# One attention-and-routing kernel: score groups moved together, mask diagonals split, routing moved, a float32 gather for two rows, dummy matmuls

## The chip, the cores and the metric

The kernel runs on one core of a Trainium2 chip. The metric is the device time of one execution in microseconds; before and after are compared by medians of several runs. All times in the rows below come from one profiled execution of the kernel before.

## The reference, cut to what matters

Three layers follow one another. Linear attention with decay, 2 batches, 8 heads, 768 tokens, 48 channels; a routed layer with 8 experts; a gated layer.

```python
# attention, per token t
cur = einsum('bhd,bhe->bhde', u * k_t, v_t);  y_t = einsum('bhd,bhde->bhe', r_t, state + cur)
state = w * state + einsum('bhd,bhe->bhde', k_t, v_t)
# experts: x = y as 1536 x 384
e = argmax(x @ w_gate);  gate_w = softmax(x @ w_gate)[e]
disp[e, position of the token among those of e] = x
out = gate_w * (relu(disp @ w1[e]) @ w2[e])
# gated layer
(sigmoid(out @ w_gate2) * (out @ w_val)) @ w_out
```

## The kernel before, in words

**Attention** works in eight steps `s`, one for each batch and pair of heads (s = 0 to 3 are batch zero, 4 to 7 batch one), over 768 tokens in six chunks of 128. The schedule is written out by hand: every engine runs its own instructions in the order of the program, and the loop `for s in range(8)` interleaves the work of several steps. In the turn `s` of the loop stand

- `a_mm(s+1, C0)` and `a_mm(s+1, C1)`: the scores of chunks 0 to 3 and 4 to 5 on PE, into two PSUM buffers (`ap`);
- `u_pe(s+1)`: products of decayed keys (`kkd`, made on POOL by `kk_part`) with values, on PE; `u_scan(s+1)`: the scan over chunks on DVE, which gives the states `ts`;
- `a_cp(s+1, ...)`: a predicated copy on DVE of the scores above the diagonal into the matrix `at`;
- `sums(s+2)`: the diagonal's values `dl` on DVE, from products that POOL makes (`pr_part`); `diag(s+2, js)`: for each of twelve 128x128 blocks an ACT instruction that writes identity times `dl` into `at`;
- `rp(s+2)` and `kb(s+2)`: the scaling of queries and keys (`dm`) on DVE, which the scores of the next turn need;
- `y_part(s, 2)`, `y_part(s+1, 0)`, `y_part(s+1, 1)`: outputs of two chunks each on PE, from the states and from `at`; `out_evac`: their copy from PSUM to `yt` on ACT;
- `out_tr(s)`: transposition and gate logits on PE (six float32 matmuls of 136 columns, which the trace shows as twelve instructions); `out_x(s)`: copy of the transposed rows to `xs` on ACT; `out_l()`: addition of the logits to `lg` on DVE.

PSUM tiles named `big` rotate through three buffers: each turn takes four, `T1[s]`, `Y0[s+1]` and two `XP[s]`.

**Expert weights** are split into a high and a low part beside the attention: `bg(n)` takes n tiles `raw`, ACT makes `rh`, DVE makes `rl`. `BG` says how many in which turn. The rest follows in the expert stage.

**Routing.** `r1(b)` finds the expert of each token (maxima, differences, one-hot `oh` on DVE, an exponential `ex` on ACT, whose sum DVE takes), `cnt` counts, `r2(b)` ranks by small matmuls on PE, `r3(b)` makes positions and gates on DVE, `r4(b, c, eng)` scales 128 rows on DVE or ACT and scatters them from POOL's queue into the buffer `xs_d` in DRAM, by expert. Batch zero is routed in the turns 4 to 6 (`RS` says which rows are sent when). After the loop, `pre()` loads the rows of expert 0 that came from batch zero, behind all six scatters of batch zero, on SP's queue; batch one is routed, and `first()` gathers expert 0's rows of batch one straight from SBUF: `xr` is transposed by PE into `xk`, and then each of six row blocks, scaled and split into a high and a low float32r part (`hi` on ACT, `lo` on DVE), is multiplied by a selection matrix `pick` and added into `xk`. `xk` is split into `xeh` and `xel`, and the expert stage begins with `s1` (`ph`).

`warm_up(n)` issues n matmuls of zeros, 512 columns each.

**Behind it** the expert stage (`s1`, `s2`) and the gated layer (`mf`, `mo`) follow; the decoding of the gated layer's weights (`wa`) runs beside them.

Of the kernel before, what the change touches and what calls it, by code (L numbers as in the profile page):

```python
# [27 lines left out]
R4E = "vsvsvs"  # L28
W0 = 3
WD = 15  # L30
ZI = (0, 0, 2, 2, 2, 2, 0, 0)
NKR = 3
NV = 4
ND = 5
WARM = 22
BG = (0, 0, 1, 1, 1, 0, 2, 3)
DP = 2
NB = 224
NP = NB // 2
OB = 6  # L40
# [6 lines left out]
OVP = 60  # L47
NT = 2
TAILF = 2
R4A = [3, 5]  # L50
R4S = [3]
EB0 = (5, 6)
EB = (4, 6)
DMAX = (122880.0 - 2.0 ** -7) * 2.0 ** 16
# [54 lines left out]
def body(tc, A, out):  # L109
    nc = tc.nc  # L110
    E = mybir.EngineType
    with ExitStack() as top, tc.manual_schedule():
# [129 lines left out]
        with ExitStack() as ctx:  # L242
# [116 lines left out]
            def diag(s, js):  # L359
                at_tile(s)  # L360
                for j in js:
                    nc.scalar.mul(AT[s][:, j, :], ident, DL[s][:, j:j + 1])  # L362

            def u_pe(s):
                for c in range(5):
                    for h in range(2):
                        nc.tensor.matmul(ups[64 * h:64 * h + 64, s % 2, :, c], kkd[s % 2][:, c, h, :],
                                         V[s][:, (2 * c + h) * 48:(2 * c + h) * 48 + 48], start=True, stop=True)
# [6 lines left out]
            def a_mm(s, cs):  # L375
                ap = ps.tile([128, 2, 512], F32, tag="a", name="ap")[:, :, 0:128 * len(cs)]
                for i, c in enumerate(cs):
                    t = slice(c * 128, c * 128 + 128)
                    for h in range(2):
                        q = slice(64 * h, 64 * h + 48)  # L380
                        nc.tensor.matmul(ap[:, h, i * 128:i * 128 + 128], D[s][q, 1, t], D[s][q, 0, t], start=True, stop=True,
                                         skip_group_check=True)
                return ap
# [34 lines left out]
            def out_evac(s, g):  # L418
                if g == 0:
                    yts[s] = wp.tile([128, 768], F32, tag="yt", name="yt")  # L420
                if s == 7:
                    a, b, src = ((0, 256, y7.get(0)), (256, 512, y7.get(1)), (512, 768, T1.get(7)))[g]
                else:
                    a, b, src = ((0, 512, Y0[s]), (512, 768, T1.get(s)))[g]
                nc.scalar.copy(out=yts[s][:, a:b], in_=src[:, 0:b - a])
# [89 lines left out]
            def first():  # L515
                x, m2, oh, rank, pi, gk = R[1]
                xk = [pb.tile([128, 512], F32, tag="big", name="xk")[:, 0:NB] for _ in range(3)]
                for b in range(2):
                    for kt in range(3):
                        nc.tensor.matmul(xk[kt][:, b * NP:b * NP + NP], xr0[0][0:NP, b, kt * 128:kt * 128 + 128],  # L520
                                         ident[0:NP, 0:NP], start=(b == 0), stop=False, skip_group_check=True)
                pick = wp.tile([128, 12, 128], F32R, tag="at", name="pick", bufs=3).rearrange("p a b -> p (a b)")
                his = wp.tile([128, 12, 128], F32R, tag="at", name="his", bufs=3).rearrange("p a b -> p (a b)")
                los = wp.tile([128, 12, 128], F32R, tag="at", name="los", bufs=3).rearrange("p a b -> p (a b)")
                for c in range(6):
                    (nc.gpsimd if c > DP else nc.vector).tensor_scalar(
                        out=pick[:, c * NB:c * NB + NB], in0=cat[:, 512:512 + NB], scalar1=pfs[1][:, c:c + 1],
                        scalar2=None, op0=ALU.is_equal)
                hl = []
                for c in range(6):  # L530
                    if c < 4:
                        hi, lo = his[:, c * 384:c * 384 + 384], los[:, c * 384:c * 384 + 384]
                    else:
                        hi = xp_.tile([128, 384], F32R, tag="hi", name="hi", bufs=2)
                        lo = xp_.tile([128, 384], F32R, tag="lo", name="lo", bufs=2)
                    hl.append((hi, lo))
                    nc.scalar.mul(hi, x[:, c, :], gk[:, c:c + 1])
                    if c in R4A:
                        r4(1, R4A.index(c), "s")
                    nc.vector.scalar_tensor_tensor(out=lo, in0=x[:, c, :], scalar=gk[:, c:c + 1], in1=hi.bitcast(F32),  # L540
                                                   op0=ALU.mult, op1=ALU.subtract)
                order = [(c, kt, p) for b in (0, 2) for p in range(2) for c in (b, b + 1) for kt in range(3)]
                order += [(c, kt, p) for kt in range(3) for c in (4, 5) for p in range(2)]
                for c, kt, p in order:
                    nc.tensor.matmul(xk[kt], hl[c][p][:, kt * 128:(kt + 1) * 128], pick[:, c * NB:c * NB + NB],
                                     start=False, stop=(c == 5 and p == 1), skip_group_check=True)
                for c in range(len(R4A), 6):
                    r4(1, c, "s" if c in R4S else "v")
                for kt in range(3):
                    nc.scalar.copy(out=xeh[:, kt, :], in_=xk[kt])  # L550
                    nc.vector.tensor_sub(xel[:, kt, :], xk[kt], xeh[:, kt, :].bitcast(F32))

            def r4(b, c, eng):
                x, m2, oh, rank, pi, gk = R[b]
                if eng == "v":
                    nc.vector.tensor_scalar_mul(x[:, c, :], x[:, c, :], gk[:, c:c + 1])
                else:
                    nc.scalar.mul(x[:, c, :], x[:, c, :], gk[:, c:c + 1])
                scatter(scx, "scx", xs_d, pi[:, c:c + 1], x[:, c, :], 8 * 1536)

            def cnt(b):
                with nc.allow_low_precision("counts of at most six are exact"):
                    nc.vector.reduce_sum(out=cnts[:, b, :], in_=R[b][2].rearrange("p c e -> p e c"), axis=AX.X)
# [4 lines left out]
            def consts():  # L568
                nc.gpsimd.tensor_copy(out=tri, in_=cat[:, 0:128])
                nc.gpsimd.memset(ones, 1.0)  # L570
                nc.gpsimd.iota(tid, pattern=[[128, 12]], base=0, channel_multiplier=1)
                nc.gpsimd.tensor_copy(out=capf, in_=capi)
# [66 lines left out]
            y_part(0, 0)  # L639
            y_part(0, 1)  # L640
            out_evac(0, 0)

            for s in range(8):
                nx, fu = s < 7, s < 6
                fetch(sum(BG[:s + 2]))
                if s < 5:
                    load(s + 3, "k")
                    load(s + 3, "v")
                if s < 4:
                    load(s + 4, "d")  # L650
                for _ in range(ZI[s]):
                    zinit()
                if s == 4:
                    consts()
                if nx:
                    ap0 = a_mm(s + 1, C0)
                    u_pe(s + 1)
                if s == 5:
                    r2(0)
                y_part(s, 2)  # L660
                out_evac(s, 1 if nx else 2)
                subs = []
                bg(BG[s], False, 0, subs)
                if nx:
                    a_cp(s + 1, C0, ap0)
                    u_scan(s + 1)
                    ap1 = a_mm(s + 1, C1)
                    a_cp(s + 1, C1, ap1)
                for c in RS.get((s, 0), ()):
                    r4(0, c, R4E[c])  # L670
                if fu:
                    sums(s + 2)
                    diag(s + 2, range(12))
                for f in subs:
                    f()
                if fu:
                    rp(s + 2)
                    behind(kk_part(s + 2), kb(s + 2))
                    if s < 5:
                        pr_part(s + 3, P_)  # L680
                if s == 4:
                    r1(0)
                    cnt(0)
                if s == 5:
                    r3(0)
                if nx:
                    y_part(s + 1, 0)
                    if s == 6:
                        out_evac(7, 0)
                    y_part(s + 1, 1)  # L690
                    out_evac(s + 1, 1 if s == 6 else 0)
                    out_tr(s)
                    out_x(s)
                    out_l()
                    for c in RS.get((s, 1), ()):
                        r4(0, c, R4E[c])
            out_tr(7)
            out_x(7, True)
            pre()
            r1(1)  # L700
# [314 lines left out]
```

## Time and profile before

| | us |
|---|---|
| runs shown: median, lowest, highest | 473.31, 471.04, 473.49 |
| the profiled execution: its time, its span | 473.62, 471.9 |
| first score matmul of turn 0 (`a_mm(1)`) | 19.52 |
| the same in turns 1, 2, 3, 4, 5, 6 | 31.76, 39.59, 47.96, 55.91, 63.94, 77.51 |
| `xr` there, first matmul on it | 94.86 |
| first matmul of the expert stage | 103.07 |

How to read the rows: a row of the timeline has start and length in us, the engine, the line, the operation, what it writes and reads, the shape, how many instructions are merged, and in brackets how long the engine had been idle before it and who released it. Engines' instructions are pipelined, so a row's length is a little more than the distance to the next row. A row of stages has its bounds, its length, then the busy time and the count of PE, PE's weight loads, DVE, ACT and POOL, then the clock that was granted to PE as a share of 2.4 GHz (0.50 is 1.2 GHz), the busy share of the DMA engines, and GB/s. SPq is SP's DMA queue, with the moment of issue.

### The profile page before, as it was taken

The page shows a single profiled execution, that of the slowest core. Times are in us where ns is not written, and L with a number is a line of the kernel's source. Part 1 is how long each engine was busy: PE and PEld are TensorE (multiplying, and loading weights), DVE is VectorE, ACT ScalarE, POOL GpSimd, SP SyncE. Part 2 cuts the span into 40 slices and gives each one's busy share as a digit, 9 for nine tenths or more (in the row PEclk, how much of TensorE's full clock was granted, in tenths as well). Part 3 has the DMA queues.
Part 4 walks back from the last instruction along what each step waited for, and adds up shares of the span by engine and source line. Part 5 has one row for each costly group of instructions (what it writes and reads, how often), then busy time and mean ns, then how long its engine had stood idle before and what let it go on. Part 6 is the DMA issues. An engine that isn't in the chain of part 4 may idle for free.

```text
span 471.9 us, 8275 instructions
## 1 busy us (share of the span) xinstructions
PE 447.4 (95%) x3210; PEld 420.0 (89%) x3211; DVE 279.7 (59%) x504; ACT 218.0 (46%) x468; POOL 108.3 (23%) x103
## 2 busy tenths in 40 slices
PE   8899979499999999999999999999999999999994
PEld 4577857499999999999988999999899999999993
DVE  6747697748998999877277767675451212121211
ACT  3346756736776767775254443434243222222222
POOL 2533543570011101200023635313104000000013
PEclk9969997879999999999999999999999999999998
DMA  7999940468798788685023533522002000000002
GB/s 242 339 293 314 312 145 19 139 241 265 216 305 241 239 266 250 162 252 192 1 68 73 129 73 129 122 79 68 1 0 102 0 2 0 1 0 1 0 4 97
DMA packets 23194, 63.53 MB, mean 135 GB/s; under 512 B 4592, under 2 KB 8304, under 8 KB 23152
## 3 DMA queue, kind: packets, MB, share of 16 engines
q1 hardware_dynamic: 21088, 58.24, 40.9%
q0 software_dynamic: 1920, 4.73, 2.7%
q8 instruction: 26, 0.43, 0.4%
q14 instruction: 16, 0.13, 0.1%
q10 hardware_dynamic: 144, 0.00, 0.0%
HBM read 55.48 MB, written 7.48 MB: 133 GB/s over the span
## 4 chain that ended last, share of the span: by engine, by line
PE 29%; DVE 12%; ACT 7%; issue 4%; POOL 1%; POOLq 0%; ACTq 0%; DVEq 0%
PE pg L940 9%; PE po L963 9%; PE pv L940 9%; DVE sg L948 2%; DVE wa L175 2%; ACT wa L165 2%; DVE wa L168 2%; DVE wa L179 2%; ACT gh L949 1%; DVE wa L171 1%; DVE gl L950 1%; ACT rh L185 1%; PE ph L840 1%; ACT sg L946 1%; PE py L859 1%
## 5 line engine op out<-in xcount | busy, mean ns | idle before, releaser
L948 DVE TENSOR_TENSOR sg<-sg,pv 128x384 f32<-128x384 f32 (+2 forms) x49 | 26.7, 544 | 91.9 <-PE pv L940 78.7
L145 DVE TENSOR_TENSOR rl<-raw,rh 128x768 fp32r<-128x768 f32 x56 | 57.1, 1020 | 11.4 <-ACT rh L143 11.4
L859 PE MATMUL py<-hh,rh 128*128 128x448 f32 x192 | 63.5, 374 | 0.0
L949 ACT CAST gh<-sg 128x384 fp32r<-128x384 f32 (+2 forms) x49 | 24.8, 507 | 80.6 <-DVE sg L948 79.1
L143 ACT CAST rh<-raw 128x768 fp32r<-128x768 f32 x64 | 53.2, 836 | 16.0 <-PE py L859 12.0
L858 PE MATMUL py<-hh,rl 128*128 128x224 f32 x192 | 52.4, 273 | 0.0
L189 POOL TENSOR_TENSOR wy<-wa,wy 128x768 fp32r<-128x768 f32 x10 | 18.8, 1878 | 143.6 <-ACT wy L185 143.6
L946 ACT ACTIVATE sg<-pg 128x384 f32<-128x384 f32 x48 | 23.4, 488 | 50.6 <-PE pg L940 50.6
L950 DVE TENSOR_TENSOR gl<-sg,gh 128x384 fp32r<-128x384 f32 (+2 forms) x49 | 28.1, 574 | 28.1 <-ACT gh L949 26.9
L211 POOL DMA_INDIRECT out_dram<-ob,ids x12 | 11.7, 975 | 120.2 <-ACT ob L970 117.8
L859 PEld LDWEIGHTS py<-hh,rh 128*128 128x128 f32 x192 | 36.4, 189 | 2.0
L858 PEld LDWEIGHTS py<-hh,rl 128*128 128x128 f32 x192 | 36.8, 192 | 0.0
L963 PE MATMUL po<-wy,gh 128*128 128x384 f32 x144 | 36.7, 335 | 0.0
L842 ACT ACTIVATE hh<-ph 128x224 fp32r<-128x224 f32 x64 | 22.8, 358 | 23.0 <-PE ph L840 20.4
L362 ACT ACTIVATE at<-cst,dl 128x128 f32<-128x128 f32 x84 | 25.4, 388 | 16.0 <-DVE dl L348 16.0
L843 DVE SCALAR_TENSOR_TENSOR hh<-ph,hh 128x224 fp32r<-128x224 f32 x64 | 24.4, 384 | 9.8 <-ACT hh L842 9.5
L840 PE MATMUL ph<-xeh,rh 128*128 128x224 f32 x96 | 26.5, 277 | 0.1
L840 PE MATMUL ph<-xh,rl 128*128 128x224 f32 x96 | 26.4, 275 | 0.0
L840 PE MATMUL ph<-xh,rh 128*128 128x224 f32 x96 | 26.1, 272 | 0.3 <-PEq L734 0.3
L840 PE MATMUL ph<-xl,rh 128*128 128x224 f32 x96 | 26.2, 273 | 0.0
L840 PE MATMUL ph<-xeh,rl 128*128 128x224 f32 x96 | 26.1, 275 | 0.0
L963 PEld LDWEIGHTS po<-wy,gh 128*128 128x128 f32 x144 | 26.0, 188 | 0.0
(199 smaller groups left out, 1213.6 us busy)
## 6 DMA issues: line engine op xcount, KB each, us to landing
raw<-in_wx_dram SPq DMA_DIRECT2D x64, 384.0 KB, 4.1
r<-in_wy_dram SPq DMA_DIRECT2D x18, 768.0 KB, 5.1
dm<-in_dm_dram SPq DMA_DIRECT2D x8, 672.0 KB, 13.2
kt<-in_kr_dram SPq DMA_DIRECT2D x8, 576.0 KB, 8.4
xs_d<-zero SPq DMA_DIRECT2D x8, 336.0 KB, 6.0
xr<-xs_d SPq DMA_DIRECT2D x8, 336.0 KB, 5.8
v<-in_v_dram SPq DMA_DIRECT2D x8, 288.0 KB, 12.5
cat<-in_cax_dram SPq DMA_DIRECT2D x1, 404.0 KB
```

The costliest lines, as they stand in the source:

```text
L143: nc.scalar.copy(out=h, in_=t)
L145: (nc.gpsimd if pool else nc.vector).tensor_sub(rl[n % NR], t, h.bitcast(F32))
L362: nc.scalar.mul(AT[s][:, j, :], ident, DL[s][:, j:j + 1])
L840: nc.tensor.matmul(ph, a[:, w], b[:, kt, :], start=(i == 0), stop=(i == 8))
L858: nc.tensor.matmul(y[:, 0, :], wl[:, w], h[:, 0, :], start=(f == 0), stop=False, skip_group_check=True)
L859: nc.tensor.matmul(y, wh[:, w], h, start=False, stop=(f == 7), skip_group_check=True)
L940: nc.tensor.matmul(pg[g], w[a][:, q], x[b][:, kt, :], start=(kt == 0 and (a, b) == (0, 0)), stop=(kt == 2 and b == 1))
L946: nc.scalar.activation(out=sg, in_=pg[0], func=AF.Sigmoid)
L948: nc.vector.tensor_mul(gg[:, a:b], sg[:, a:b], pg[1][:, a:b])
L949: nc.scalar.copy(out=gh[:, a:b], in_=gg[:, a:b])
L950: nc.vector.tensor_sub(gl[:, a:b], gg[:, a:b], gh[:, a:b].bitcast(F32))
L963: nc.tensor.matmul(po[i], g[v][:, a], w[u][:, q], start=(f == 0 and (u, v) == (0, 0)), stop=(f == 11 and v == 1))
```

## The change

- `warm_up(6)` is added ahead of the loop, `warm_up(7)` behind `out_tr(7)`.
- `a_mm(s+1, C1)` goes ahead of `u_pe(s+1)`, except in turns 5 and 6, where it stays behind `u_scan`.
- `out_l()` goes from the end of a turn to behind `u_scan` of the next one (in turn 6 there is one at the end as well).
- `diag(s+2)` is split: blocks 0 to 7 where all twelve were, blocks 8 to 11 behind `out_evac` and `out_x` at the end of the turn.
- Batch zero's `r1(0)` and `cnt(0)` go from behind `kb(6)` and `pr_part(7)` to ahead of the weight splits and `rp(6)`; `r2(0)` from turn 5 to the end of turn 4; `r3(0)` from the end of turn 5 to behind its `u_scan` and `out_l`.
- `BG` has seven tiles in place of eight: one in turns 2 and 3, none in turn 4, five in turn 6, none in turn 7.
- In `first()` all six `pick` are made on DVE (before, three on POOL). Row blocks 0 and 1 are scaled by `r4` first and gathered by one float32 matmul for each column block; blocks 2 to 5 keep the high and low parts. The scalings of 2 to 5 go to ACT and DVE in turn.

```diff
@@
+WE = 6
+WF = 7
-BG = (0, 0, 1, 1, 1, 0, 2, 3)
-DP = 2
+BG = (0, 0, 1, 1, 0, 0, 5, 0)
-R4A = [3, 5]
-R4S = [3]
@@ first()
-                for c in range(6):
-                    (nc.gpsimd if c > DP else nc.vector).tensor_scalar(
-                        out=pick[:, c * NB:c * NB + NB], in0=cat[:, 512:512 + NB], scalar1=pfs[1][:, c:c + 1],
-                        scalar2=None, op0=ALU.is_equal)
-                hl = []
-                for c in range(6):
-                    if c < 4:
-                        hi, lo = his[:, c * 384:c * 384 + 384], los[:, c * 384:c * 384 + 384]
-                    else:
-                        hi = xp_.tile([128, 384], F32R, tag="hi", name="hi", bufs=2)
-                        lo = xp_.tile([128, 384], F32R, tag="lo", name="lo", bufs=2)
-                    hl.append((hi, lo))
+                def choose(c):
+                    nc.vector.tensor_scalar(out=pick[:, c * NB:c * NB + NB], in0=cat[:, 512:512 + NB],
+                                            scalar1=pfs[1][:, c:c + 1], scalar2=None, op0=ALU.is_equal)
+
+                choose(0)
+                r4(1, 0, "v")
+                r4(1, 1, "s")
+                choose(1)
+                for c in range(2):
+                    for kt in range(3):
+                        nc.tensor.matmul(xk[kt], x[:, c, kt * 128:(kt + 1) * 128], pick[:, c * NB:c * NB + NB].bitcast(F32),
+                                         start=False, stop=False, skip_group_check=True)
+                hl = {}
+                for c in range(2, 6):
+                    choose(c)
+                    o = (c - 2) * 384
+                    hl[c] = hi, lo = his[:, o:o + 384], los[:, o:o + 384]
                     nc.scalar.mul(hi, x[:, c, :], gk[:, c:c + 1])
-                    if c in R4A:
-                        r4(1, R4A.index(c), "s")
...
-                order = [(c, kt, p) for b in (0, 2) for p in range(2) for c in (b, b + 1) for kt in range(3)]
+                order = [(c, kt, p) for p in range(2) for c in (2, 3) for kt in range(3)]
...
-                for c in range(len(R4A), 6):
-                    r4(1, c, "s" if c in R4S else "v")
+                for c in range(2, 6):
+                    r4(1, c, "sv"[c % 2])
@@ ahead of the loop
+            warm_up(WE)
@@ the loop
+                late = s in (5, 6)
                 if nx:
                     ap0 = a_mm(s + 1, C0)
+                    if not late:
+                        ap1 = a_mm(s + 1, C1)
                     u_pe(s + 1)
-                if s == 5:
-                    r2(0)
...
                     a_cp(s + 1, C0, ap0)
                     u_scan(s + 1)
-                    ap1 = a_mm(s + 1, C1)
+                out_l()
+                if s == 5:
+                    r3(0)
+                if nx:
+                    if late:
+                        ap1 = a_mm(s + 1, C1)
                     a_cp(s + 1, C1, ap1)
...
                     sums(s + 2)
-                    diag(s + 2, range(12))
+                    diag(s + 2, range(8))
+                if s == 4:
+                    r1(0)
+                    cnt(0)
                 for f in subs:
                     f()
...
-                if s == 4:
-                    r1(0)
-                    cnt(0)
-                if s == 5:
-                    r3(0)
...
                     out_tr(s)
                     out_x(s)
-                    out_l()
+                    if s == 6:
+                        out_l()
+                    if fu:
+                        diag(s + 2, range(8, 12))
+                    if s == 4:
+                        r2(0)
...
             out_tr(7)
+            warm_up(WF)
             out_x(7, True)
```

## Rows read from the trace of the kernel before

**Rows 1.** Busy time by stage of the span, PE's granted clock near the end.

```profile
19.50:31.75 12.25, 11.77 (x100) 9.11 (x100) 5.65 (x8) 5.96 (x19) 7.71 (x7) 0.61 1.03 314
31.75:47.96 16.21, 15.51 (x201) 12.79 (x201) 11.09 (x16) 9.25 (x29) 4.74 (x7) 0.98 1.00 294
47.96:55.91 7.95, 7.70 (x102) 6.26 (x101) 6.07 (x9) 5.70 (x18) 3.99 (x4) 1.00 0.98 328
55.91:63.94 8.03, 7.70 (x102) 6.26 (x101) 6.12 (x10) 5.78 (x18) 4.65 (x8) 1.00 0.88 291
63.94:77.51 13.57, 10.83 (x108) 8.45 (x107) 11.21 (x22) 7.12 (x23) 5.42 (x5) 0.75 0.05 20
87.94:94.86 6.92, 0.48 (x12) 0.41 (x12) 6.58 (x23) 5.17 (x11) 3.34 (x4) 0.68 0.51 166
94.86:103.07 8.21, 8.21 (x49) 8.21 (x49) 3.84 (x9) 3.46 (x8) 6.83 (x7) 0.64 0.74 275
103.07:221.80 118.73, 118.36 (x922) 115.19 (x920) 102.12 (x191) 81.24 (x163) 12.43 (x8) 1.00 0.79 240
```

**Rows 2.** Timeline of PE in turn 0.

```profile
19.52 1.16 PE L381 MATMUL ap<-dm 48*128 48x128 f32 x16 [1.47 <-issue]
21.14 0.79 PE L367 MATMUL ups<-v,kkd 128*64 128x48 f32 x20 [0.45 <-POOL kkd L335]
28.74 3.09 PE L432 MATMUL xp<-cat,yt 128*128 128x136 f32 x12
```

**Rows 3.** Timeline of PE in turn 3.

```profile
54.30 1.66 PE L432 MATMUL xp<-cat,yt 128*128 128x136 f32 x12
```

**Rows 4.** Timeline of DVE in turn 3.

```profile
49.67 0.47 DVE L457 TENSOR_TENSOR lg<-lg,xp 128x24 f32<-128x24 f32 x2 [1.85 <-ACT xs L446]
50.06 1.31 DVE L386 COPY_PREDICATED at<-msk,ap 128x1024 f32<-128x1024 uint8 x1
51.27 0.63 DVE L371 TENSOR_TENSOR_SCAN ts<-wsc,ups 112x240 f32<-112x240 f32 x1
54.90 0.95 DVE L340 TENSOR_TENSOR dm<-dm,ft 112x768 f32<-112x768 f32 x1
```

**Rows 5.** Timeline of ACT, turns 3 and 6.

```profile
53.28 3.33 ACT L362 ACTIVATE at<-cst,dl 128x128 f32<-128x128 f32 x11 [0.94 <-DVE dl L348]
...
81.10 1.57 ACT L143 CAST rh<-raw 128x768 fp32r<-128x768 f32 x2
...
85.44 0.62 ACT L558 ACTIVATE xs<-xs,gkp 128x384 f32<-128x384 f32 x1
```

**Rows 6.** Timeline of DVE, batch zero's first routing part.

```profile
66.88 1.20 DVE L472 TENSOR_TENSOR oh<-eq,m 128x48 bf16<-128x48 f32 x1
...
68.54 0.20 DVE L563 TENSOR_REDUCE cnts<-oh 128x8 bf16<-128x48 bf16 x1
```

**Rows 7.** Timeline of POOL, turns 0 and 6.

```profile
22.54 1.41 POOL L331 TENSOR_TENSOR pr<-pr,cat 128x576 f32<-128x576 f32 x1
...
82.62 1.44 POOL L211 DMA_INDIRECT xs_d<-xs,pi  x1 [0.59 <-DVE xs L556]
84.37 0.97 POOL L211 DMA_INDIRECT xs_d<-xs,pi  x1 [0.30 <-issue]
...
87.64 1.70 POOL L211 DMA_INDIRECT xs_d<-xs,pi  x1 [0.31 <-ACT rh L143]
```

**Rows 8.** Timeline of PE, routing of both batches and gather.

```profile
68.14 0.20 PE L486 MATMUL rk<-oh,tri 128*128 128x48 bf16 x1 [2.12 <-DVE oh L472]
...
94.86 2.87 PE L520 MATMUL xk<-cst,xr 112*128 112x112 f32 x12 [2.72 <-DMA xr<-xs_d]
97.41 1.60 PE L545 MATMUL xk<-pick,his 128*128 128x224 f32 x6
...
102.95 0.28 PE L545 MATMUL xk<-pick,lo 128*128 128x224 f32 x1
```

**Rows 9.** Timeline of SP's DMA queue, the load of expert 0's rows.

```profile
91.22 0.33 SPq L513 DMA_DIRECT2D xr<-xs_d  x1
```

## The prediction

> **What bounds the kernel now.** I read the stages first. From 103 us on PE is busy 118.36 of 118.73 us in the expert stage, at full clock [rows 1], and the change alters almost nothing there (one weight tile more is split, early). So what counts is when the expert stage begins: 103.07. I take what lies behind as rigid. Ahead of it the time is made of turns, and the turns differ.
>
> In turn 0 PE is busy 11.77 of 12.25 us, but at a mean clock of 0.61; in the turns up to 5 the mean is 0.98 to 1.00; in turn 5 it is 0.75, and from 88 to 103 us 0.68 and 0.64 [rows 1]. In turn 0 the fall comes after two idle gaps, 1.47 and 0.45 us, and out_tr then takes 3.09 us where it takes 1.66 at full clock [rows 2, 3]. In turn 5 it comes after a gap of 2.12 us, in which PE waits for the one-hot matrix; then 2.72 us more are waited for xr [rows 8].
>
> In a warm turn (3), PE is busy 7.70 of 7.95 us [rows 1], but a cycle over ACT and DVE is as long: sums, twelve diagonals (0.303 us each [rows 5]), the evacuation, the xs copies, then on DVE the logits, which have waited 1.85 us for ACT, the copy of scores, the scan [rows 4]. PE has only 0.25 us of waits left, so breaking that cycle can give no more than this per turn.
>
> **The change, part by part.** Times are counted from the turn's first score matmul, as T.
>
> *Turn 0, dummies and both score groups.* Six dummies of 512 columns (1.4 us by the estimate used for the gather, below) fill the 1.47 us gap at the front, and the second score group (0.6 us) fills the 0.45 us in which PE waited for POOL's keys [rows 2]. If this keeps the clock up, the turn costs the 7.7 us of a warm one. Is anything else late then? POOL's product ends at 22.54 + 1.41 = 23.95 [rows 7]; from there sums, rp and kb on DVE take 2.5 us, to 26.45, and PE would be ready for the next scores at 19.52 + 7.7 = 27.2: PE decides. So turn 1 begins at 27.2 in place of 31.75: **−4.55**. Lower bound of the gain: the clock falls anyway, and only the 0.45 us go.
>
> *Turns 1 to 3, logits and diagonals.* Without the wait for ACT, the scan starts when u_pe is done, which stands behind both score groups: T + 2.7. From the scan's start to kb's end the old turn 3 takes 51.27 to 55.85, 4.6 us with a weight split in it [rows 4]; the logits put 0.47 into it; so kb ends at T + 7.8 in turns 2 and 3, which have a split, and PE needs 7.7 in turn 1. That is 23.3 for three turns, against 55.91 − 31.75 = 24.16 [rows 1]: **−0.9**. Splitting the diagonals costs nothing: eight are done at T + 7.5, ahead of the next predicated copy, and the last four at about T + 10, which is 2 us into the next turn, whose copy of the second group stands at 3.8. XP's buffers are held longer by the logits, which are read at T + 3.75; the first output matmuls that want one come just then. Cost zero, but without reserve.
>
> *Turn 4, routing of batch zero ahead of rp and kb.* Here something is added. Behind sums (end T + 5.1) DVE now runs r1(0). Its three slow operations (the one-hot one took 1.20 us [rows 6]) ran beside POOL's products before and shall take about 0.2 each, as POOL is idle then. But the sum of the exponentials waits for ACT, and there the exponential is queued behind eight diagonals: 5.1 + 8 x 0.303 + 0.24 = T + 7.8. Behind it on DVE: four short operations of about 0.2 us, as the count in [rows 6], then rp and kb, 1.8 us: kb ends at T + 10.45, and the scores of turn 5 start there, at 10.5 in place of 8.03 [rows 1]: **+2.5**. PE is done at T + 8.2 with its ranks and has a gap of 2.3 us.
>
> *Turn 5.* The wait for the one-hot matrix goes from here, and r3 stands behind the logits; a_mm of the second group waits about 0.5 us for r3's reading of the ranks' buffer. So a warm turn takes 7.7 + 0.1 + 0.5 = 8.3. But the gap of 2.3 us in front of it is as long as the one of 2.12 after which the clock fell before, and longer than turn 0's [rows 2, 8]. A clock of 0.75 over 13.57 us is 6.8 us at half [rows 1]; work that takes 3.09 cold takes 1.66 warm, so 6.8 us cost 2.9. Turn 5 then takes 11.2 against 13.57: **−2.4** (bounds: −5.3 with the clock up, −1.4 if it stays low for 9 us).
>
> *Turn 6, five splits.* ACT: evacuation to T + 3.6, five rh at 0.78 (two took 1.57 [rows 5]) to 7.5, one scaling 0.6, two evacuations 0.86, two copies 0.7, the last scaling 0.6: T + 10.2, where it ended at 86.06 − 77.51 = 8.55 [rows 5]. The last two scatters follow, 0.97 + 0.30 each [rows 7]: the second ends at T + 12.85. From a scatter's end to xr's issue took 91.22 − 89.34 = 1.9 [rows 7, 9], so xr is issued at T + 14.7 in place of 13.7: **+1.0**. What is saved in turn 7 (three splits in front of the logits) is given to nobody: even before, the positions were there 2 us ahead of xr, and now they have 4.5 us of cover.
>
> A rule speaks against this part. The five DVE splits run behind the five rh, from T + 4.8 to 9.3 without a pause, and two scatters fall among them. In the trace a scatter beside two splits took 1.44 us, and one beside three 1.70, where an undisturbed one takes 0.97 [rows 7]: it squeezes in, and both are done ahead of the last two, so I charge nothing. The Trainium skill (SBUF — State Buffer, section "SBUF: two separate sides") says that a DMA from GpSimd's queue starves wholly while VectorE holds the port they share. By that rule the two scatters would wait until 9.3, four would follow one another, and xr would be 1.5 us later; the sum would be −1.8 in place of the one below.
>
> *Gather.* Seven dummies (about 0.24 us each at full clock, an estimate from the 0.11 of 224 columns [rows 8]) begin behind the last out_tr at T + 11.2 and end at 12.9, with the ranks' start; the ranks end at 13.3; xr lands 3.64 us after its issue [rows 8, 9], at 18.4. That leaves 5 us without work for PE, more than any gap after which the clock stood. So I take the gather as cold at first, as now: 0.64 over 8.21 us [rows 1] is 5.9 us at half clock. The transposes take 2.55 cold (94.86 to 97.41 [rows 8]). Two blocks lose 12 float32r matmuls (0.11 each warm, up to the last at 102.95; 0.23 cold, six from 97.41 to 98.81 [rows 8]) and get 6 in float32, two instructions each: 0.134 us for 136 columns warm (1.61 for 12 [rows 3]), so 0.20 to 0.22 for 224; cold 0.40. Then 3.35 us of the cold time hold 8 of the 12 instructions, the rest takes 0.7, and 24 float32r 2.65: 9.3 in place of 8.2: **+1.1** (bounds: 6.3, −1.9, if all is warm; +1.4 if the clock comes back later). DVE's 1.5 us saved by the missing low parts, and POOL's three slow picks that vanish, lie under the wait for xr.
>
> **Sum**: −4.55 − 0.9 + 2.5 − 2.4 + 1.0 + 1.1 = −3.3. The profiled execution took 473.62, which becomes 470.3; it stood 0.3 over the median of the runs shown, so I forecast **470.0**.
>
> **Rivals.**
>
> *The gap in turn 4 leaves the clock up.* Turn 5 then costs 8.3: −6.2, 467.1. For it: the gap is split between waits, and in turn 3, with 0.25 us of waits, the clock stood [rows 1]. Against: after 1.47 + 0.45 us it fell [rows 2].
>
> *The clock falls in turn 0 all the same.* Gain there 0.5 in place of 4.55: sum +0.8, 474.1. Against: PE has hardly an idle moment left before the place of the fall. For: the dummies end just as the scores begin, and a late kb(1) would open the gap again.
>
> *The dummies do bridge the gap.* If xr comes earlier than I reckon, or the clock falls late, the gather is warm: 3.0 less, 467.0. It needs xr within about 2 us of the ranks; I count 5.
>
> *Slower: the clock, once down in turn 4, stays down to the end of turn 6.* After turn 0's fall the clock was down for the rest of the turn (0.61 [rows 1], out_tr at 3.09 [rows 2]). If it goes so here, and on, turn 5 takes 13.5 cold (+2.3 on the sum), and in turn 6 PE reaches the last transposition 3.4 us later than ACT needs it: −3.3 + 5.7 = +2.4, 475.7. It decides from some 15 us at half clock on. Against: mean 0.75 in turn 5 [rows 1].
>
> *Scatters blocked by the splits:* both wait until T + 9.3, then four of 1.27 us follow one another, and the last ends at 14.4: +1.5, 471.5. It needs scatters that don't run beside splits at all, where two rows show that they do [rows 7]. It is what the Trainium skill's rule above (SBUF — State Buffer) would make of turn 6.
>
> **From these to the numbers.** Forecast 0.47 (own range 468.5 to 471.5), clock up in turn 5 0.24, fall in turn 0 0.10, dummies bridge 0.07, slower 0.06, scatters blocked 0.06. About 0.5% (2.4 us) can be told from no change: below 470.9 is faster. The forecast is so by 0.75 of its chance, the two fast rivals wholly: faster 0.68. Slower (above 475.7) has half of the slow rival and a little of the others: 0.07. Same 0.25. The range 465.6 to 473.6 leaves out most of the slow rival, over half of the fall in turn 0, and a little at the fast end.
>
> **What would show it.** Right: turn 0 at full clock, turn 1's scores at about 27.2; logits directly behind the scan; in turn 4 a DVE gap until the exponential, and PE waiting some 2.3 us for kb; five rh in a row; xr 14.7 us after turn 6's first scores; a gather that begins at half clock. Wrong: PE waiting for another thing in turn 1 (a load, an XP buffer), a clock that stays up through turn 5, xr well before or after its place, or a gain that comes back in the expert stage because weights are late.

## The result

| | before | after |
|---|---|---|
| median of 9 runs, us | 473.38 | 468.80 |
| lowest, highest | 471.03, 474.88 | 464.37, 469.69 |
| ratio of the runs, 95% interval | | 0.9897 [0.9866, 0.9929] |
| profiled execution: time, span | 473.62, 471.9 | 468.81, 467.0 |

The change made the kernel about 1% faster: 4.6 us between the medians, 4.9 between the profiled spans. The forecast was 470.0 in a range of 465.6 to 473.6.

Executions of one and the same program fall into clusters here, a few us apart, and the mean granted clock tells them apart; one profile shows one execution. That turned out to matter more than any single term, and is taken up below.

The stages of the changed kernel's span follow, with the columns of [rows 1]: turns 0, 1 to 3, 4, 5, turn 6's first scores to the first matmul on `xr`, the gather, the rest.

```profile
19.39:26.72 7.33, 7.33 (x101) 6.15 (x100) 5.20 (x7) 3.57 (x13) 4.63 (x5) 1.00 1.01 301
26.72:49.09 22.37, 22.14 (x301) 18.45 (x300) 17.01 (x26) 16.79 (x52) 11.60 (x12) 1.00 1.03 332
49.09:59.16 10.07, 7.54 (x106) 6.37 (x107) 6.76 (x17) 7.26 (x24) 4.66 (x8) 1.00 0.91 353
59.16:71.02 11.86, 11.74 (x101) 9.04 (x101) 6.38 (x13) 3.73 (x11) 6.66 (x6) 0.60 0.03 10
71.02:88.88 17.86, 12.71 (x147) 10.06 (x148) 13.73 (x38) 14.21 (x30) 6.00 (x6) 0.98 0.30 103
88.88:98.73 9.85, 9.83 (x49) 9.24 (x49) 1.43 (x5) 1.02 (x3) 5.94 (x6) 0.66 0.79 283
98.73:467.00 368.27, 358.01 (x2300) 351.33 (x2300) 209.86 (x362) 163.30 (x318) 58.92 (x42) 1.00 0.37 108
```

Turn 0 is now at full clock, and turns 1 to 3 and turn 5 are shorter too; turn 4, turn 6 and the gather take half of that back. Term by term, against the old profile, with the forecast beside it:

| | before | after | difference | forecast |
|---|---|---|---|---|
| up to turn 0's scores | 19.52 | 19.39 | −0.1 | 0 |
| turn 0 | 12.24 | 7.33 | −4.9 | −4.55 |
| turns 1 to 3 | 24.15 | 22.37 | −1.8 | −0.9 |
| turn 4 | 8.03 | 10.07 | +2.0 | +2.5 |
| turn 5 | 13.57 | 11.86 | −1.7 | −2.4 |
| turn 6's scores to xr used | 17.35 | 17.86 | +0.5 | +1.0 |
| gather | 8.21 | 9.85 | +1.6 | +1.1 |
| expert stage to the end | 368.83 | 368.27 | −0.6 | 0 |

Three timelines of the changed kernel show the places. DVE in turn 4 waits for the exponential; kb, which the next scores need (the last row), stands behind it:

```profile
54.84 0.21 DVE L471 TENSOR_TENSOR oh<-eq,m 128x48 bf16<-128x48 f32 x1
56.62 0.20 DVE L477 TENSOR_REDUCE se<-ex 128x6 f32<-128x48 f32 x1 [1.58 <-ACT ex L473]
...
57.17 0.20 DVE L565 TENSOR_REDUCE cnts<-oh 128x8 bf16<-128x48 bf16 x1
...
58.16 0.95 DVE L339 TENSOR_TENSOR dm<-dm,ft 112x768 f32<-112x768 f32 x1
```

The one-hot operation takes 0.21 us where it took 1.20 beside POOL's products [rows 6]; then 1.58 us go by until ACT is through its eight diagonals. PE, behind both:

```profile
56.37 0.27 PE L487 MATMUL rk<-oh,ones 128*128 128x40 bf16 x5
59.16 1.16 PE L380 MATMUL ap<-dm 48*128 48x128 f32 x16 [2.53 <-DVE dm L339]
...
68.00 3.09 PE L431 MATMUL xp<-cat,yt 128*128 128x136 f32 x12
...
82.54 1.67 PE L284 MATMUL wt<-zero 128*128 128x512 bf16 x6
...
88.88 2.88 PE L519 MATMUL xk<-cst,xr 112*128 112x112 f32 x12 [4.27 <-DMA xr<-xs_d]
91.55 4.49 PE L534 MATMUL xk<-pick,xs 128*128 128x224 f32 x12
95.71 0.98 PE L547 MATMUL xk<-pick,his 128*128 128x224 f32 x6
```

After the gap of 2.53 us the clock falls (0.60 over turn 5), and out_tr again takes 3.09 us. The dummies end 4.7 us ahead of xr, and the ranks behind them 4.3 us. The gather runs at half clock (0.50 to 0.51) up to 95.71 and at full clock from there, and the float32 part takes 4.16 us from its start to the next row. In turn 6, the five splits and the last scaling of rows on DVE, the last scaling on ACT, and then POOL's scatters:

```profile
76.20 4.42 DVE L146 TENSOR_TENSOR rl<-raw,rh 128x768 fp32r<-128x768 f32 x5
80.72 0.41 DVE L558 TENSOR_SCALAR xs<-xs,gkp 128x384 f32<-128x384 f32 x1
80.08 0.65 ACT L560 ACTIVATE xs<-xs,gkp 128x384 f32<-128x384 f32 x1
```

```profile
76.56 1.44 POOL L210 DMA_INDIRECT xs_d<-xs,pi  x1 [2.10 <-DVE xs L558]
79.36 1.25 POOL L210 DMA_INDIRECT xs_d<-xs,pi  x1 [1.36 <-ACT yt L424]
81.41 0.97 POOL L210 DMA_INDIRECT xs_d<-xs,pi  x1 [0.81 <-DVE xs L558]
82.69 0.97 POOL L210 DMA_INDIRECT xs_d<-xs,pi  x1 [0.30 <-ACT xs L445]
```

The first two run beside the splits (76.20 to 80.62) and take 1.44 and 1.25 us, where the last pair, which stands alone, takes 0.97 each. That pair is released by DVE's scaling, which stands behind the splits and ends at 81.13; ACT's was over at 80.73.

### The profile page after: what moved, and what is told of

Read it like the earlier page. It is cut to its first block, busy times and chain, and to the rows that moved or that the text cites. A ratio compares the mean times of both kernels' runs of the same rounds, so it can differ in the third digit from the quotient of the medians.

```text
span 467.0 us, 8303 instructions
## 1 busy us (share of the span) xinstructions
PE 447.0 (96%) x3221; PEld 419.8 (90%) x3224; DVE 274.6 (59%) x505; ACT 217.2 (47%) x466; POOL 104.3 (22%) x100
## 3 DMA queue, kind: packets, MB, share of 16 engines
HBM read 55.48 MB, written 7.48 MB: 135 GB/s over the span
## 4 chain that ended last, share of the span: by engine, by line
PE 29%; DVE 12%; ACT 7%; issue 4%; POOL 1%; POOLq 0%; ACTq 0%; DVEq 0%
PE pg L953 9%; PE po L976 9%; PE pv L953 9%; DVE sg L961 2%; DVE wa L174 2%; DVE wa L167 2%; ACT wa L164 2%; DVE wa L178 2%; ACT gh L962 1%; DVE gl L963 1%; DVE wa L170 1%; ACT rh L184 1%; PE ph L853 1%; ACT sg L959 1%; PE py L872 1%
```

## The experiments

Each is an edit of the changed kernel, where not said otherwise. Times are medians; a profile is of one execution.

**1. No dummies in front.**

```diff
-            warm_up(WE)
```

> The changed kernel without the six dummies ahead of the loop. Theory A (the dummies hold the clock, the second score group alone doesn't): PE is idle again for about 1.4 us before turn 0's scores, the clock falls in turn 0 as in the kernel before, turn 0 takes 10.5 to 12 us in place of 7.3, and the time is 472 to 473.5. Rival B (the second score group in front of u_pe closes the gap that mattered): turn 0 stays at 7.3 us and the time at 468.8 within 0.7.

Measured: 469.16, but from 462.97 to 474.8 in 6 runs. The profiled execution (467.92) kept the clock through turn 0, which took 7.42 us, behind a gap of 1.27 us:

```profile
19.37 1.61 PE L380 MATMUL ap<-dm 48*128 48x128 f32 x24 [1.27 <-issue]
20.99 0.79 PE L366 MATMUL ups<-v,kkd 128*64 128x48 f32 x20
21.71 0.72 PE L408 MATMUL y<-dm,ts 48*64 48x128 f32 x8
```

Neither theory: here the clock was kept without the dummies, and the time goes with the mean clock of the run: 0.989 at 462.97, 0.978 at 467.5 and 467.9, 0.975, 0.968 and 0.965 at 470.4, 472.8 and 474.8. In the slowest of them turn 0 may well have fallen; no profile shows one.

**2. The dummies in front alone,** in the kernel before.

```diff
             out_evac(0, 0)
+            warm_up(6)
```

> The kernel before with nothing but six dummies ahead of the loop. Theory A: turn 0 runs at full clock and takes 8 to 8.5 us in place of 12.2 (the waits of 0.45 us and for the scan stay), the rest is as before: 469 to 470. Rival B: the 0.45 us wait for POOL's keys still lets the clock fall, and the time is 473.4 as before.

Measured: 469.20, from 468.21 to 470.07 in 12 runs, ratio 0.9953 [0.9924, 0.9983]. The 0.45 us wait for POOL's keys is 0.21 here, and turn 0 takes 7.81 us at full clock in place of 12.24:

```profile
19.44 1.16 PE L381 MATMUL ap<-dm 48*128 48x128 f32 x16
20.81 0.79 PE L367 MATMUL ups<-v,kkd 128*64 128x48 f32 x20 [0.21 <-POOL kkd L335]
...
27.25 1.16 PE L381 MATMUL ap<-dm 48*128 48x128 f32 x16
```

On the same chip the kernel before lay at 468.2 to 470.3 in 11 of 23 runs (mean clock 0.976 to 0.978) and at 472.5 to 474.3 in the others (0.965 to 0.969). The dummies take the slower cluster away. They make nothing faster than the kernel before is in its better executions. And 469.20 is within 0.4 us of the whole change (468.80, on another occasion): what the six dummies give in front is all that the change gives, and its other parts add up to nothing.

**3. The exponential ahead of the diagonals** of turn 4.

```diff
                     sums(s + 2)
-                    diag(s + 2, range(8))
                 if s == 4:
                     r1(0)
                     cnt(0)
+                if fu:
+                    diag(s + 2, range(8))
```

> The changed kernel with batch zero's r1 and count written ahead of the eight diagonals of turn 4, so that ACT makes the exponential first and DVE does not wait for it. Theory A (the wait for the exponential makes turn 4's gap, and the gap lowers the clock in turn 5): turn 4 takes 8.4 to 8.8 us in place of 10.1, PE's gap shrinks from 2.5 to about 1 us, turn 5 stays at full clock with 7.8 to 8.5 us in place of 11.9, and the time is 463 to 464. Rival B (the gap goes, but the clock falls all the same, from the small matmuls of the ranks or of r3): only 1.5 us are won, 467.3. Rival C: the diagonals, now 0.9 us later, hold up turn 5's predicated copy, and what is won goes there: 468.5.

Measured: 461.37 (460.62 to 465.23), ratio 0.9801 [0.9747, 0.9855], better than theory A. The timeline of PE, and turn 5 and the gather as stages:

```profile
57.45 1.16 PE L380 MATMUL ap<-dm 48*128 48x128 f32 x16 [0.89 <-DVE dm L339]
60.70 0.72 PE L380 MATMUL ap<-dm 48*128 48x128 f32 x8
65.19 1.16 PE L380 MATMUL ap<-dm 48*128 48x128 f32 x16
```

```profile
57.45:65.19 7.74, 7.61 (x101) 6.23 (x101) 6.24 (x13) 4.23 (x15) 4.55 (x5) 1.00 0.18 66
82.55:90.57 8.02, 8.02 (x49) 7.87 (x49) 1.88 (x6) 1.21 (x3) 5.83 (x6) 0.79 0.90 323
```

Turn 4 takes 57.45 − 49.02 = 8.43, turn 5 stays at full clock with 7.74. In this execution the clock was also up for more of the gather (0.79 in place of 0.66), which gave 1.8 us more; that was not expected. The mean clock was 0.989 to 0.992 in five of the six runs.

**4. Nineteen dummies in the wait for xr.**

```diff
+                warm_up(19)
                 xk = [pb.tile([128, 512], F32, tag="big", name="xk")[:, 0:NB] for _ in range(3)]
```

> The changed kernel with nineteen more dummies between batch one's ranks and the transposes of xr, about 4.1 us at full clock, in the 4.3 us in which PE waits for xr. Theory A (the gather is slow because the clock falls in that wait): the gather takes 6.2 to 6.6 us from xr to the expert stage in place of 9.85, and the time is 465 to 466. Rival B (the gather is paced by DVE's low parts or ACT's high ones): it stays above 8 us and the time above 467.5. Rival C: the dummies run past the landing of xr and give back what they win, up to 0.5 us.

Measured: 473.87 (467.63 to 475.8), slower than the changed kernel, and the edit was to blame. The profile is of one of three faster executions (467.6 to 468.4, mean clock 0.991 to 0.994); the other nine, at 473.5 and more (0.973 to 0.980), have none. `xr` lies in the buffer of the tile `zero`, which the dummies read, so its load had to wait for them. SP's queue and PE:

```profile
84.45 0.32 SPq L513 DMA_DIRECT2D xr<-xs_d  x1
```

```profile
80.16 4.26 PE L285 MATMUL wt<-zero 128*128 128x512 bf16 x19
87.74 1.56 PE L521 MATMUL xk<-cst,xr 112*128 112x112 f32 x12 [3.31 <-DMA xr<-xs_d]
```

The load is issued when the dummies end (80.16 + 4.26), 5.1 us behind the last scatter; a new gap of 3.31 us follows, and the clock falls in the gather all the same (0.79 over 8.04 us). What it tells besides: this execution had a gap of 2.52 us ahead of turn 5 as well, and yet turn 5 took 7.72 us at full clock:

```profile
59.33 1.16 PE L381 MATMUL ap<-dm 48*128 48x128 f32 x16 [2.52 <-DVE dm L340]
...
67.05 1.16 PE L381 MATMUL ap<-dm 48*128 48x128 f32 x16
```

**5. The same with the identity matrix in place of zeros.**

```diff
+            def warm_id(n):  # as warm_up, z = ident.bitcast(BF16), 256 columns
...
+                warm_id(38)
                 xk = ...
```

> The changed kernel with 38 dummies of 256 columns on the identity matrix (4.1 us at full clock) between batch one's ranks and the transposes of xr. In the run with nineteen dummies on the tile of zeros, xr, which lies in that tile's buffer, was issued only when they had ended, 5.1 us behind the last scatter in place of 1.9; the identity has no such tie. Theory A (the gather is slow because the clock falls in the wait for xr): xr stays at 17.9 us behind turn 6's first scores, the gather takes 6.2 to 6.6 us in place of 9.85, and the time is 465 to 466. Rival B (the gather is paced by ACT or DVE): above 8 us, 467.5 or more. Rival C (the clock falls in spite of the dummies, or the remaining gap is enough): no change, 468.8.

Measured: 465.92 (461.12 to 467.06), ratio 0.9847 [0.9795, 0.9899].

```profile
84.56 4.31 PE L290 MATMUL wt<-cst 128*128 128x256 bf16 x38
88.90 1.56 PE L526 MATMUL xk<-cst,xr 112*128 112x112 f32 x12
90.30 2.45 PE L541 MATMUL xk<-pick,xs 128*128 128x224 f32 x12
92.42 0.99 PE L554 MATMUL xk<-pick,his 128*128 128x224 f32 x6
```

xr comes at 17.45 us behind turn 6's scores (17.86 in the changed kernel), the gather ends at 95.25, after 6.35 us, and the float32 part takes 2.12 in place of 4.16. Theory A.

**6. All six blocks in float32r.**

```diff
-                r4(1, 0, "v"); r4(1, 1, "s")     # and the float32 matmuls of blocks 0 and 1
+                for c in range(6):               # hi and lo for all, scalings behind the gather
```

> The changed kernel with all six row blocks gathered in float32r with a high and a low part, none in float32. Theory A (at half clock the float32 gather of two blocks costs PE more than what it saves on DVE and ACT, which wait for xr anyway): the twelve instructions that take 4.2 us become twelve of 0.23, 2.8 us, and the gather takes 8.3 to 8.9 us in place of 9.85; the time is 467.6 to 468. Rival B (DVE's low parts become the bound): the first high part is multiplied late, and the gather takes 9.5 us or more, 468.5 to 469.5.

Measured: 467.32 (462.71 to 467.43), ratio 0.9868 [0.982, 0.9917]. The gather runs from 88.59 to 97.23, 8.64 us: theory A.

```profile
88.59 2.87 PE L519 MATMUL xk<-cst,xr 112*128 112x112 f32 x12 [4.03 <-DMA xr<-xs_d]
...
97.23 0.97 PE L849 MATMUL ph<-xeh,rh 128*128 128x224 f32 x3
```

The float32 gather alone costs 1.2 us (9.85 against 8.64), both with the clock at half at first.

**7. Experiments 3, 5 and 6 together.**

> The changed kernel with the exponential ahead of the diagonals, 38 dummies on the identity in the wait for xr, and all six blocks in float32r. If the three act on different waits: turns 4 and 5 as in the run with the exponential first (461.4), the gather at full clock in 5.2 to 5.6 us in place of 9.85 or, in that run, 8.0: 458 to 459. Rival: with a warm gather DVE's low parts, which are made from about 85 us on in any case, become the bound; then 459.5 to 460.5.

Measured: **459.46**, all 6 runs within 459.32 to 459.77, ratio 0.9725 [0.9686, 0.9763]. The clock stays at full from turn 0 on.

```profile
78.55 4.31 PE L290 MATMUL wt<-cst 128*128 128x256 bf16 x38
83.04 1.56 PE L526 MATMUL xk<-cst,xr 112*128 112x112 f32 x12 [0.18 <-DMA xr<-xs_d]
...
88.47 0.97 PE L857 MATMUL ph<-xeh,rh 128*128 128x224 f32 x3
```

The gather takes 5.43 us: the three act on different waits. (Of the 6.35 of experiment 5, float32 thus cost 0.9.) The time is still 0.5 above the forecast, because the rest of the span takes 369.4 us in place of 368.3: PE waits 0.88 us for the rows of expert 1 at 99.0, a wait that the changed kernel's trace does not have. The next limit shows.

**8. The logits back at the end of the turn.**

```diff
-                out_l()
                 if s == 5:
                     r3(0)
...
-                    if s == 6:
-                        out_l()
+                    out_l()
```

> The changed kernel with the logits at the end of each turn again, ahead of the next turn's predicated copy. Theory A (the copy then waits for ACT's xs, as in the kernel before): turns 1 to 3 take 7.9 to 8.1 us in place of 7.3 to 7.5, and the time is 470 to 470.5. Rival B (with only eight diagonals ahead of the evacuation ACT is early enough, and the move of the logits gave nothing): turns stay at 7.3 to 7.5, 468.8.

Measured: 468.44 (467.89 to 470.19), no difference. Turns 1 to 3 take 49.28 − 26.91 = 22.37, to the hundredth as with the move. Rival B.

**9. The diagonals whole again.**

```diff
-                    diag(s + 2, range(8))
+                    diag(s + 2, range(12))
...
-                    if fu:
-                        diag(s + 2, range(8, 12))
```

> The changed kernel with all twelve diagonals ahead of the evacuation again, and the logits still behind the scan. Theory A (splitting the diagonals is what lets ACT's copies come early enough): turns 1 to 3 take 7.9 to 8.1 us in place of 7.3 to 7.5, and the time is 470 to 470.5. Rival B (with the logits behind the scan the copy of scores waits for nothing on ACT but the diagonals): turns stay at 7.3 to 7.6, but in turn 4 the exponential waits for four diagonals more, 1.2 us, so 470.

Measured: 470.86 (469.63 to 472.89). Turns 1 to 3 take 49.34 − 26.97 = 22.37 again; turn 4 takes 11.24 in place of 10.07. Rival B, with the price in turn 4.

**10. Both undone.**

> The changed kernel with twelve diagonals ahead of the evacuation and the logits at the end of each turn. Theory A (the cycle sums, diagonals, evacuation, xs, logits, copy, scan bounds the old turns, and either of the two moves breaks it): turns 1 to 3 take 7.8 to 8.1 us in place of 7.3 to 7.5, and the exponential comes 1.2 us later: 471.5 to 472. Rival B (what shortened the turns is the second score group ahead of u_pe, not these two): turns stay at 7.3 to 7.6, 470.

Measured: 472.57 (472.02 to 473.9). Turns 1 to 3 take 51.21 − 26.83 = 24.38. DVE in turn 3, where the old wait is back:

```profile
45.00 0.47 DVE L456 TENSOR_TENSOR lg<-lg,xp 128x24 f32<-128x24 f32 x2 [1.85 <-ACT xs L445]
45.39 1.31 DVE L385 COPY_PREDICATED at<-msk,ap 128x1024 f32<-128x1024 uint8 x1
```

Theory A, with turns a little longer than it said (8.13): either move alone breaks the cycle, and the second one then gives nothing in these turns. With neither, the joined score groups shorten nothing either: the old kernel took 24.15.

**11. The second score group late in all turns.**

```diff
-                late = s in (5, 6)
+                late = True
```

> The changed kernel with the second score group behind the scan in all turns. Theory A (PE sets the turns, and its 24 score matmuls in one go are only a little shorter than in two): turns 1 to 3 take 7.6 to 7.8 us, turn 0 8.0, and the time is 470 to 470.5. Rival B (the second group's early scores are what freed DVE): turns take 7.9 us or more, 471 or more.

Measured: 471.37 (467.02 to 474.06). Turns 1 to 3 take 51.04 − 27.51 = 23.53, turn 0 27.51 − 19.55 = 7.96, 0.36 of it a wait for POOL's keys. Between the theories: 7.84 a turn is just above A's size, and the time is B's. Both play a part: on PE 24 scores take 1.54 us in one go (19.39 to 20.93 in the changed kernel) and 1.09 + 0.64 in two, 0.2 more, and turns 3 and 4 begin 0.29 us late, behind kb:

```profile
42.94 1.16 PE L380 MATMUL ap<-dm 48*128 48x128 f32 x16 [0.29 <-DVE dm L339]
...
51.04 1.16 PE L380 MATMUL ap<-dm 48*128 48x128 f32 x16 [0.29 <-DVE dm L339]
```

**12. No dummies behind the last transposition.**

```diff
-            warm_up(WF)
```

> The changed kernel without the seven dummies behind the last transposition. Theory A (they end four us ahead of xr and can't hold the clock for the gather): the gather takes 9.5 to 9.9 us as with them, and the time is 468.8 within 0.5. Rival B (they keep the clock up so much longer that it comes back earlier): the gather takes 10.5 us or more, 469.6 to 470.5.

Measured: 468.74 (464.72 to 469.72), no difference. The ranks wait 1.47 us where the dummies stood, and xr's matmuls begin at half clock as before. Theory A.

## Why the prediction was right

The sum was right in its main term and in its sign; that it came out so near is partly luck, as the terms were off by 0.4 to 0.9 us in both directions.

**What bounds the kernel.** Right: the change moved the start of the expert stage from 103.07 to 98.73, 4.3 us. The rest of the span is 0.6 shorter, but no gain of the change: in experiment 2, where that stage is the old one, it took 368.33 too.

**Turn 0.** The mechanism held in the profiled execution, and the term was 0.35 too small, because I took PE's busy time of the old warm turn, 7.7 us, for the new turn's length; from first score to first score it is 7.33. The 24 score matmuls in one go give 0.2 of that (experiment 11); the rest is not taken apart.
What the step did not see is that the old fall is no property of the program. Experiment 2 shows it: the old kernel runs at the dummies' time in about half of its executions. That turn 0 keeps the clock in these is inferred, as none was profiled: what turn 0 lost, 0.39 of 12.25 us, is 1% of the span, the difference between mean clocks of 0.968 and 0.978. The forecast was made from a profile of the other half, and the runs that it was compared with were mostly of that half too, which was luck. Against a better mix (472.49, 473.36 and 470.88 were its medians on later occasions) the gain is smaller, and against its better executions (468.2 to 470.3) there is none.

**Turns 1 to 3.** Right in direction, but the forecast was half of the −1.8 measured. Turn 1 is PE's, and the same 7.7 is the mistake there. Turns 2 and 3 are kb's, as forecast, but kb ended at T + 7.44 and 7.48, not 7.8; in turn 3:

```profile
48.09 0.95 DVE L339 TENSOR_TENSOR dm<-dm,ft 112x768 f32<-112x768 f32 x1
49.09 1.61 PE L380 MATMUL ap<-dm 48*128 48x128 f32 x24
```

The limit of 0.25 us a turn was wrong as well: it took PE's work as given, and turn 3 lost 0.42. The two moves without the joined score groups give 0.62 in the three turns (23.53, experiment 11), within that limit; the joined groups without the moves give nothing (24.38, experiment 10); both together give 1.8. And I gave the gain to both moves, but one would have done (experiments 8 to 10). The second is a spare.

**Turn 4.** The step held in each link: fast one-hot operation, wait for the exponential (1.58 us), kb late, a gap on PE (2.53 forecast as 2.3). Experiment 3 takes the wait away by order alone.

**Turn 5.** Half clock, as forecast, 11.86 against 11.2, but two sizes offset each other: a clock of 0.60 over 11.86 us is 9.5 us at half, not 6.8, while a warm turn takes 7.7 (experiments 3 and 4), not 8.3, as the wait of 0.5 us for r3 does not occur. (By its own ratio, 1.66 to 3.09, the prediction's 6.8 us cost 3.1, not 2.9.) The rival with the clock up is no rival but another execution of the same program: one of nine runs of the changed kernel took 464.37 at a mean clock of 0.987, against 0.977 to 0.980 for the rest, and experiment 4's profile shows such a turn 5 with the same gap. I had given it 0.24.

**Turn 6.** +0.5 in place of +1.0; xr was issued at T + 14.5 and landed sooner, 3.35 us behind its issue and not 3.64. The path was another than the prediction's: the last scatters waited for DVE's scaling behind the five splits (81.13), not for ACT's, where the evacuations took 0.63, not 0.86. The two scatters beside the splits took 0.3 to 0.5 us longer than alone and were not held to the end of all five: the first was over at 78.00, with three splits to go. The second ended with the last split (80.61), so it decides nothing.
The Trainium skill (SBUF — State Buffer, section "SBUF: two separate sides") says that GpSimd can't write a DMA's descriptors while VectorE runs an operation in a two-port mode, and names a float32 copy as one. I applied it to splits, which are subtractions of two inputs, so these rows show how scatters fare beside such splits, and don't test the rule.

**Gather.** The half clock was forecast, and the term was 0.5 too small: the transposes took 2.67 us (forecast 2.55), the 12 float32 instructions 4.16 (4.05), and the float32r part up to the expert stage 3.02 (2.65). The nearness of the float32 part is luck: the clock stayed at half for 6.8 us, not 5.9, so that all 12 instructions ran at half clock, but each took 0.35 us there, not 0.40. Experiments 5 and 6 separate the two causes: clock 3.5 us, float32 1.2. The dummies behind the last transposition give nothing (experiment 12), as they end 4.7 us ahead of xr. The gain in DVE and ACT that float32 brings lies under that wait, as the step said.

## What to carry to other kernels

Profile several executions, or look at the mean granted clock of each run, before a stall of the clock is counted as a gain: an edit that fills a gap may only remove the worse of two clusters. An instruction that one engine needs from another is best written ahead of the other's long batch: the exponential ahead of eight diagonals was worth more than the whole change (7.4 us against 4.6; in the profile the wait itself is 1.6 of it, and the clock behind it the rest). Where two edits break the same cycle, count the gain once. And dummies must stand in the gap itself, and must not read a buffer that the awaited load writes.

## What was not expected of the hardware

A gap of about 2.5 us on PE left the clock up in one execution (experiment 4) and was followed by half clock in another (the changed kernel); a gap of 1.27 us was harmless in experiment 1's profile, where runs of the same program spread over 12 us. In experiment 7, whose profile has gaps of 0.9 us and less, all 6 runs lay within 0.45 us.

Scatters that run beside splits end with a split, in both kernels: at 78.00 and 80.61 where a split ends at 78.02 and 80.62, and before at 84.06 and 89.34 where one ends at 84.08 and 89.36. Each took 0.3 to 0.7 us more than the 0.97 of one that stands alone.
